# Two score pairs ahead of the last key tile's values, in front of six blocks of an attention and feed-forward kernel

## The chip, the cores and the metric

The kernel runs on one core of one Trainium2 chip. The metric is the device time of one execution in microseconds (us); less is better. Before the change the median of three runs is 1400.2 us (1399.88 to 1400.24).

## What is computed

Layer normalisation of x (2048 tokens, 512 features), softmax attention with 32 heads of 16 features on it, a gated feed-forward network of width 1792 on the same normalised x, and a gated sum. All data are 32-bit floats.

```python
def _A_ref(x, wqkv, wo):
    B, S, D = x.shape
    H = 32; Dh = D // H
    qkv = (lambda x, *d: x.transpose(*d))((x @ wqkv).reshape(B, S, 3, H, Dh), 2, 0, 3, 1, 4)
    q, k, v = qkv[0], qkv[1], qkv[2]
    scale = Dh ** -0.5
    scores = jnp.einsum("bhqd,bhkd->bhqk", q, k) * scale
    p = _softmax(scores, axis=-1)
    o = jnp.einsum("bhqk,bhkd->bhqd", p, v)
    return (lambda x, *d: x.transpose(*d))(o, 0, 2, 1, 3).reshape(B, S, D) @ wo

def _B_ref(x, w_gate, w_up, w_down):
    g = _silu(x @ w_gate)
    u = x @ w_up
    return (g * u) @ w_down

x = A_x
xn = _layernorm(x, axis=-1)
s = _A_ref(xn, A_wqkv, A_wo)
g = _silu(_B_ref(xn, B_w_gate, B_w_up, B_w_down))
return x + s * g
```

## The kernel before

**Stages.** A prologue normalises x and projects it to queries, keys and values. Then the attention runs for 32 units, each of one group of four heads and one block of 512 queries over 16 key tiles of 128 keys. A unit is cut into blocks of three to six key tiles, 101 blocks in all, counted here from 0. The feed-forward network, and after it most of the output projection, are cut into small portions that are laid between the attention's instructions. A short end finishes the last query block.

**One block** (`run`, from line 957 on) has two parts. In the first part, called the stage here, TensorE makes the block's scores and works off the block's share of feed-forward portions. In the second part, the values' stretch, it multiplies the probabilities with the values. The order is written out on the host: `events` gives each block a list of steps D, A, B and F at set places, `run` issues them in that order, and every engine then works through its own queue in order.

- **D** is a direct score pair (`scored`, lines 944 to 949): two matmuls, one on rows 0 to 63 of the array and one on rows 64 to 127, into the two halves of one of two score buffers (line 942), and an exponential on ScalarE from that buffer into a probability tile `pr` (line 948). Since there are two buffers, the third D has to wait for the exponential of the first, and so on. Each key tile has two pairs.
- **A and B** are the two halves of a copied score pair: one matmul into the spare bank `acc[1]` (also line 942, in the profile with the output `acc`), and a VectorE copy out of it into the probability tile (line 1001 for A, line 1007 for B). There is one spare bank, so each of these matmuls waits for the copy in front of it. The exponential of a copied pair comes at the end of the stage, from the probability tile (line 1015).
- **F** is one feed-forward pair (`fill(1)`): a matmul on each half of the array, into `bankx` and `banky` (`both`, line 188). A block gets 24 such pairs where the gate and up projections are at work and 21 (`3 * FG`) where the down projection is, until the feed-forward network is done at block 86 (`early` is 87); later blocks get 12 or 9.
- **Values** (`values`, line 405): for each key tile four matmuls, one per head, each with a stationary operand of 128 x 17 and an output at its own quarter of the partitions of `acc[0]`. The profile records each of them as two, so a key tile is x8 in its rows.

From block 87 on, `run` already uses another end: it issues the values of all key tiles but the last, then `begin` (the first two D of the next block), and then the values of the last key tile. The next block finds those two pairs in `begun` and leaves its first two D out of its list. In blocks 0 to 85 all values come first and the two D open the next block.

VectorE also has chores (splitting weights and hidden values into two parts, normalising finished units). `run` issues a chore after a step where its planned cost fits ahead of the next copy.

A block of six key tiles with 24 feed-forward pairs has 10 D and 2 copied pairs. One with 21 feed-forward pairs has 9 D and 3 copied pairs; its steps are D D F A F F F F D B F F D F F A F D F F F D B F F D F A F F D F F B D F. There are six such blocks: 7, 19, 40, 52, 73 and 85, each the second block of its unit. The block in front of each has five key tiles.

Of the kernel before, what the change touches and what calls it, by code (L numbers as in the profile page):

```python
# [33 lines left out]
FG = 7  # L34
# [18 lines left out]
def tile_block(ctx: ExitStack, tc: tile.TileContext, x, wqkv, wo, w_gate, w_up, w_down, out):  # L53
# [87 lines left out]
    def tidy(room=None):  # L141
        while chores and (room is None or chores[0][0] <= room):
            cost, work = chores.pop(0)
            work()
            if room is not None:
                room -= cost
# [19 lines left out]
    def catch_up():  # L166
        while after:
            after.pop(0)()
# [30 lines left out]
    def close():  # L199
        while closing:  # L200
            closing.pop(0)()
# [136 lines left out]
    def out_steps():  # L338
        if now == early:
            for c in range(DT - 1):  # L340
                load_out(0, c)
        if now == early + 1:
            for c in range(DT - 1):
                load_out(1, c)
            for t in range(NT):
                load_gates(t)
        if now == opened[units - 3] + 3:
            for c in range(DT - 1):
                load_out(2, c)
        if now == opened[units - 1] + 1:  # L350
            load_gate()

    def out_splits():
        for b, c in {early + 1: ((0, 0), (0, 1)), early + 2: ((0, 2),), early + 3: ((1, 0),), early + 4: ((1, 1),),
                     early + 6: ((1, 2),), early + 7: ((2, 0),), early + 8: ((2, 1),), early + 10: ((2, 2),)}.get(now, ()):
            split_out(b, c)
        if now - opened[units - 1] - 2 in range(EARLY):
            gate_rest(now - opened[units - 1] - 2)
# [42 lines left out]
    def values(u, kts, probs):  # L401
        for kt in kts:
            v = vst[(u // NB * NB + kt // CT) % RING]
            for h in range(4):
                mm(acc[0][h * 32:h * 32 + DH + 1], v[:, kt % CT, h * (DH + 1):(h + 1) * (DH + 1)],  # L405
                   probs[kt, h // 2][:, h % 2], start=kt == 0, stop=kt == KT - 1, skip_group_check=True)
# [59 lines left out]
    now = -1  # L466

    def fill(n):
        nonlocal given
        while n > 0 and queue:  # L470
            next(queue[0][0])
            queue[0][1] -= 1
            if not queue[0][1]:
                queue.pop(0)
            n -= 1
            given += 1

    sizes = []
# [4 lines left out]
    sizes = sizes[1:] + [3 * (DT - 1)] * EARLY + [3 * DT] * (NB * NT - NT)  # L483
    early = len(sizes) - EARLY - (NB * NT - NT)

    blocks, opened = [], []
# [19 lines left out]
    def events(n, f):  # L506
        length = 2 * n + f
        need = 2 * n - max(2, (10 * length + 46) // 40)
        fit = (10 * length + 55) // 112
        copied = max(0, min(need, fit)) if now else 0  # L510
        direct = 2 * n - copied
        gap = max(4, min(5, (length - 8) / max(1, direct - 2)))
        marks = [(0, "D"), (1, "D")] + [(7 + gap * i, "D") for i in range(direct - 2)]
        marks += [(2.2 + max(5.6, min(8, (length - 5) / (2 * copied))) * i, "AB"[i % 2]) for i in range(2 * copied)]
        marks.sort(key=lambda mark: mark[0] - 0.6 * (mark[1] == "D"))
        out = []
        at = left = 0
        for t, kind in marks:
            while left < f - (kind != "D") and at < t:
                out.append((at, "F"))  # L520
                left += 1
                at += 1
            out.append((at, kind))
            at += 1 if kind == "D" else 0.5
        return direct, out + [(at + i, "F") for i in range(f - left)]
# [409 lines left out]
    now = 0  # L935
# [3 lines left out]
    def scores(u, bank, kt, j, h):  # L939
        k, kc = kst[(u // NB * NB + kt // CT) % RING], kt % CT  # L940
        r = slice(h * HALF, h * HALF + NROW)
        mm(bank, k[r, j, kc * P:(kc + 1) * P], qst[u % 2][r, j], start=True, stop=True)  # L942

    def scored(u, slot, kt, j):
        for h in order():
            scores(u, score[slot][:, h], kt, j, h)
        pr = ppool.tile([P, 2, TB], F32, tag="pr", name="pr")
        act(pr, score[slot], AF.Exp, scale=0.25)  # L948
        return pr
# [3 lines left out]
    def begin(u, first, n):  # L953
        for j in range(2):
            begun[first, j] = scored(u, j, first, j)

    def run(u, first, n):
        nonlocal lower
        f = sizes.pop(0) if sizes else 0
        direct, todo = events(n, f)  # L960
        if now == 0:
            for _ in range(4):
                todo.insert(0, todo.pop(max(i for i, (_, e) in enumerate(todo) if e == "F")))
        pairs = [(kt, j) for kt in range(first, first + n) for j in range(2)]
        straight, copies = pairs[:direct], pairs[direct:]
        probs, waiting, turned_in = {}, [], []

        def unit_end():
            while ends:
                ends.pop(0)()  # L970
            out_steps()

        done = len(begun)
        if done:
            probs.update(begun)
            begun.clear()
            todo = [i for i in todo if i not in ((0, "D"), (1, "D"))]
            unit_end()
        copying = [t + 1.5 for t, e in todo if e in "AB"]
        final = max(at for at, (_, e) in enumerate(todo) if e == "F")  # L980
        free = 0
        for at, (t, e) in enumerate(todo):
            if at == final and not copying:
                tidy()
            if e == "F":
                fill(1)
            elif e == "D":
                probs[straight[done]] = scored(u, done % 2, *straight[done])
                done += 1
                if done == 2:  # L990
                    unit_end()
            elif e == "A":
                if now > early + 1 and not turned_in:
                    turned_in.append(now)
                    out_splits()
                kt, j = copies.pop(0)
                waiting.append((kt, j))
                scores(u, spare_bank, kt, j, 0)
                lower = True
                probs[kt, j] = ppool.tile([P, 2, TB], F32, tag="pr", name="pr")  # L1000
                dve.tensor_copy(probs[kt, j][:, 0], spare_bank)  # L1001
                free = copying.pop(0) + 3
            else:
                kt, j = waiting[-1]
                scores(u, spare_bank, kt, j, 1)
                lower = False
                dve.tensor_copy(probs[kt, j][:, 1], spare_bank)  # L1007
                free = copying.pop(0) + 3
            if not copying:
                close()  # L1010
            while chores and at < final and (not copying or max(free, t) + chores[0][0] <= copying[0] + 0.5):
                free = max(free, t) + chores[0][0]
                chores.pop(0)[1]()
        for kt, j in waiting:
            act(probs[kt, j], probs[kt, j], AF.Exp, scale=0.25)  # L1015
        tidy()
        if not turned_in:
            out_splits()
            tidy()
        catch_up()  # L1020
        kts = range(first, first + n)
        if early <= now + 1 < len(blocks):
            values(u, kts[:-1], probs)
            begin(*blocks[now + 1])
            values(u, kts[-1:], probs)
        else:
            values(u, kts, probs)

    for now, (u, first, n) in enumerate(blocks):
        g, b = divmod(u, NB)  # L1030
        if first == 0 and 0 < u < units - 1:
            load_q(u + 1)
            load_shift(u + 1)
        if now == 3 or first == 0 and 0 < g < NG - 1 and b == 0:
            load_k(g + 1, 0)
            load_v(g + 1, 0)
        run(u, first, n)
        if now == 0:
            load_k(0, NB - 1)
            load_v(0, NB - 1)  # L1040
        elif now == 1:
            load_q(1)
            load_shift(1)
        if b == NB - 1 and g + 1 < NG:
            for c in range(NB - 1):
                if first < (c + 1) * CT <= first + n:
                    load_k(g + 1, c + 1)
                    load_v(g + 1, c + 1)
        if first + n == KT and u + 1 < units:
            ends.append(partial(finish, u))  # L1050
# [81 lines left out]
```

## Time and profile before

| what | before |
|---|---|
| median of three runs | 1400.2 us (1399.88 to 1400.24) |
| the profiled execution's own time | 1399.78 us |
| its span (first to last recorded instruction) | 1398.0 us |
| granted TensorE clock, mean | 1.0 |
| TensorE matmul busy | 1391.3 us, 100% of the span |
| ScalarE busy | 1088.8 us, 78% |
| VectorE busy | 770.5 us, 55% |

In the rows, PE is TensorE's matmuls, PEld its weight loads, DVE is VectorE, ACT is ScalarE, POOL is GpSimd. L942 is line 942 of the kernel. A row of the timeline gives the start in us, the length in us, the engine, the line, the operation, output<-inputs with their shapes, and how many instructions were merged; in brackets stands how long the engine was idle before and who released it. TensorE's matmuls are pipelined and a new one starts before the last has ended, so a busy share of 100% does not say that nothing waits: one has to look at the distance from start to start.

### The profile page before, as it was taken

The page shows a single profiled execution, that of the slowest core. Times are in us where ns is not written, and L with a number is a line of the kernel's source. Part 1 is how long each engine was busy: PE and PEld are TensorE (multiplying, and loading weights), DVE is VectorE, ACT ScalarE, POOL GpSimd, SP SyncE. Part 2 cuts the span into 40 slices and gives each one's busy share as a digit, 9 for nine tenths or more (in the row PEclk, how much of TensorE's full clock was granted, in tenths as well). Part 3 has the DMA queues.
Part 4 walks back from the last instruction along what each step waited for, and adds up shares of the span by engine and source line. Part 5 has one row for each costly group of instructions (what it writes and reads, how often), then busy time and mean ns, then how long its engine had stood idle before and what let it go on. Part 6 is the DMA issues. An engine that isn't in the chain of part 4 may idle for free.

```text
span 1398.0 us, 27683 instructions
## 1 busy us (share of the span) xinstructions
PE 1391.3 (100%) x11193; PEld 842.4 (60%) x11193; DVE 770.5 (55%) x1301; ACT 1088.8 (78%) x1245; POOL 90.8 (6%) x104
## 2 busy tenths in 40 slices
PE   9999999999999999999999999999999999999998
PEld 7777755655665565566556556655565565565554
DVE  6674555455645653556446645554565446556555
ACT  6753678877888877787888778778877887788885
POOL 4200200000000000000000000000000000000333
PEclk9999999999999999999999999999999999999999
DMA  7768741043634511254514303356224123234433
GB/s 228 271 243 259 185 103 43 13 116 85 131 85 118 118 43 36 56 132 95 138 50 112 91 13 73 77 145 148 60 72 114 34 46 73 66 88 141 125 100 112
DMA packets 126954, 148.14 MB, mean 106 GB/s; under 512 B 12524, under 2 KB 79340, under 8 KB 126052
## 3 DMA queue, kind: packets, MB, share of 16 engines
q1 hardware_dynamic: 121620, 125.79, 35.1%
q0 software_dynamic: 4912, 20.12, 3.9%
q8 instruction: 89, 1.46, 0.4%
q14 instruction: 45, 0.37, 0.1%
q10 hardware_dynamic: 288, 0.39, 0.1%
HBM read 106.68 MB, written 39.58 MB: 105 GB/s over the span
## 4 chain that ended last, share of the span: by engine, by line
PE 88%; ACT 0%; DVE 0%; issue 0%; DVEq 0%
PE acc L405 32%; PE bankx L188 23%; PE score L942 17%; PE banky L188 12%; PE acc L942 3%; ACT pr L948 0%; PE acc L1069 0%; PE banky L1069 0%; PE score L1069 0%; DVE y L1076 0%; DVE y L1082 0%; DVEq L1128 0%
## 5 line engine op out<-in xcount | busy, mean ns | idle before, releaser
L948 ACT ACTIVATE pr<-score 128x1024 f32<-128x1024 f32 x856 | 810.4, 1031 | 228.5 <-PE score L942 226.3
L405 PE MATMUL acc<-pr,vst 128*17 128x512 f32 x4096 | 461.9, 593 | 0.0
L942 PE MATMUL score<-qst,kst 50*128 50x512 f32 x1712 | 391.0, 413 | 0.1
L188 PE MATMUL bankx<-fx,guh 64*128 64x512 f32 x896 | 333.5, 393 | 0.1
L188 PE MATMUL banky<-fx,guh 64*128 64x512 f32 x896 | 324.7, 393 | 0.0
L405 PEld LDWEIGHTS acc<-pr,vst 128*17 128x17 f32 x4096 | 108.7, 97 | 285.9 <-issue 262.2
L942 PEld LDWEIGHTS score<-qst,kst 50*128 50x128 f32 x1712 | 175.2, 184 | 148.1 <-issue 68.0
L1001 DVE COPY pr<-acc 128x512 f32<-128x512 f32 x168 | 116.3, 692 | 193.2 <-PE acc L942 191.4
L188 PE MATMUL bankx<-wd,hh 64*128 64x512 f32 x672 | 199.9, 392 | 0.0
L188 PE MATMUL banky<-wd,hh 64*128 64x512 f32 x672 | 197.4, 392 | 0.0
L188 PEld LDWEIGHTS bankx<-fx,guh 64*128 64x128 f32 x896 | 166.4, 186 | 18.7 <-issue 0.9
L188 PE MATMUL banky<-fx,gul 64*128 64x512 f32 x448 | 175.4, 391 | 0.0
L188 PE MATMUL bankx<-fx,gul 64*128 64x512 f32 x448 | 175.3, 391 | 0.0
L1015 ACT ACTIVATE pr<-pr 128x1024 f32<-128x1024 f32 x168 | 172.3, 1077 | 0.0
L188 PEld LDWEIGHTS banky<-fx,guh 64*128 64x128 f32 x896 | 166.4, 186 | 6.1
L1007 DVE COPY pr<-acc 128x512 f32<-128x512 f32 x168 | 116.2, 691 | 72.2 <-PE acc L942 61.3
L241 DVE SCALAR_TENSOR_TENSOR ga<-th,bankx 128x512 f32<-128x512 f32 x56 | 38.5, 688 | 178.4 <-ACT th L240 178.4
L942 PE MATMUL acc<-qst,kst 50*128 50x512 f32 x336 | 135.1, 402 | 0.0
L188 PEld LDWEIGHTS bankx<-wd,hh 64*128 64x128 f32 x672 | 125.0, 186 | 13.1
L188 PEld LDWEIGHTS banky<-wd,hh 64*128 64x128 f32 x672 | 124.4, 186 | 3.3
L188 PEld LDWEIGHTS bankx<-fx,gul 64*128 64x128 f32 x448 | 83.7, 187 | 10.3
L188 PEld LDWEIGHTS banky<-fx,gul 64*128 64x128 f32 x448 | 83.5, 186 | 3.7
(179 smaller groups left out, 1323.6 us busy)
## 6 DMA issues: line engine op xcount, KB each, us to landing
gur<-in_B_w_gate_dram SPq DMA_DIRECT2D x56, 256.0 KB
gur<-in_B_w_up_dram SPq DMA_DIRECT2D x56, 256.0 KB
wdr<-in_B_w_down_dram SPq DMA_DIRECT2D x56, 256.0 KB
kst<-k_d SPq DMA_DIRECT2D x192, 64.0 KB
qst<-q_d SPq DMA_DIRECT2D x192, 64.0 KB
fx<-xt_d SPq DMA_DIRECT2D x24, 512.0 KB
q_d<-parts SPq DMA_DIRECT2D x16, 512.0 KB
k_d<-parts SPq DMA_DIRECT2D x16, 512.0 KB
```

Source lines behind the costliest of these rows:

```text
L188: mm(banks[i], lhs[halves[i]], rhs[halves[i]], start=start, stop=stop)
L241: dve.scalar_tensor_tensor(ga, th, 1.0, bankx, op0=ALU.add, op1=ALU.mult)
L405: mm(acc[0][h * 32:h * 32 + DH + 1], v[:, kt % CT, h * (DH + 1):(h + 1) * (DH + 1)], probs[kt, h // 2][:, h % 2], start=kt == 0, stop=kt = ...
L942: mm(bank, k[r, j, kc * P:(kc + 1) * P], qst[u % 2][r, j], start=True, stop=True)
L948: act(pr, score[slot], AF.Exp, scale=0.25)
L1001: dve.tensor_copy(probs[kt, j][:, 0], spare_bank)
L1007: dve.tensor_copy(probs[kt, j][:, 1], spare_bank)
L1015: act(probs[kt, j], probs[kt, j], AF.Exp, scale=0.25)
```

## The change

The early start of the next block, used from block 87 on, is also used in front of every block of six key tiles whose share of the feed-forward work is 21 pairs.

```diff
         kts = range(first, first + n)
-        if early <= now + 1 < len(blocks):
+        if early <= now + 1 < len(blocks) or blocks[now + 1:] and blocks[now + 1][2] == 6 and sizes[0] == 3 * FG:
             values(u, kts[:-1], probs)
             begin(*blocks[now + 1])
             values(u, kts[-1:], probs)
         else:
             values(u, kts, probs)
```

It moves instructions at six places in TensorE's order, all of the same kind. The first of them, where block 6 ends and block 7 begins, stands in the following piece of the difference; `vst_549` and `vst_553` are values of key tiles 0 to 3 and of key tile 4, `score_8969` and `score_8970` are the two score buffers, and a row's x is the number of matmuls in the program.

```order
 L188 MATMUL banky<-wd,hh 128x512
 L405 MATMUL acc_80<-pr,vst_549 17x512 x16
-L405 MATMUL acc_80<-pr,vst_553 17x512 x4
 L942 MATMUL score_8969<-qst_556,kst_552 128x512 x2
 L942 MATMUL score_8970<-qst_556,kst_552 128x512 x2
+L405 MATMUL acc_80<-pr,vst_553 17x512 x4
 L188 MATMUL bankx<-wd,hh 128x512
 L188 MATMUL banky<-wd,hh 128x512
```

The four score matmuls of block 7's first two pairs now stand between the fourth and the fifth key tile's values instead of behind the fifth's.

On VectorE one place differs, in block 85. `fx<-wor` and `part<-pair` are chores, each a cast and a subtraction; `pr<-acc_81` are the copies of A (L1001) and B (L1007).

```order
 L193 SCALAR_TENSOR_TENSOR y<-th,y 128x512
 L1013 CAST fx<-wor 128x512
+L1001 COPY pr<-acc_81 128x512
 L1013 TENSOR_TENSOR fx<-wor,fx 128x512
-L1001 COPY pr<-acc_81 128x512
+L1007 COPY pr<-acc_81 128x512
 L1013 CAST part<-pair 128x512
-L1007 COPY pr<-acc_81 128x512
+L1001 COPY pr<-acc_81 128x512
 L1013 TENSOR_TENSOR part<-pair,part 128x512
-L1001 COPY pr<-acc_81 128x512
 L1007 COPY pr<-acc_81 128x512
```

The three chores behind the first cast each move back by one copy. The order of the instructions on ScalarE, GpSimd and SyncE, and so of all their DMAs, is the same as before.

## Prediction

> **What bounds the kernel now.** I begin with the page's first and fourth part, the busy times and the chain that ended last.
>
> ```profile
> PE 1391.3 (100%) x11193; PEld 842.4 (60%) x11193; DVE 770.5 (55%) x1301; ACT 1088.8 (78%) x1245; POOL 90.8 (6%) x104
> PE 88%; ACT 0%; DVE 0%; issue 0%; DVEq 0%
> ```
>
> TensorE carries 88% of the chain and no other engine 1%. So what counts is how TensorE's starts follow each other around the six places, and whether ScalarE, at 78%, holds it up there.
>
> Second view: the busy times in stretches, one for each stage, from the end of one values' stretch to the start of the next as the timeline gives them. The first six are the stages of blocks 7, 19, 40, 52, 73 and 85, which the change prepares earlier. Then come block 8 (five key tiles, 21 pairs), block 10 (six, 24 pairs) and block 11 (five, 24 pairs). The first number behind the colon pair is the length.
>
> ```profile
> 245.92:254.23 8.31, 8.31 (x67) 6.83 (x67) 3.83 (x6) 7.61 (x9) 0.00 (x0) 1.00 0.00 0
> 399.64:407.78 8.14, 8.14 (x67) 6.77 (x66) 3.81 (x6) 7.54 (x8) 0.26 (x1) 1.00 0.09 34
> 669.64:677.76 8.12, 8.12 (x67) 6.76 (x66) 3.81 (x6) 7.51 (x8) 0.13 (x1) 1.00 0.91 234
> 823.47:831.76 8.29, 8.29 (x67) 6.82 (x66) 3.81 (x6) 7.60 (x9) 0.00 (x0) 1.00 0.00 0
> 1093.42:1101.70 8.28, 8.28 (x66) 6.79 (x66) 3.81 (x6) 7.61 (x9) 0.00 (x0) 1.00 0.01 2
> 1247.21:1255.38 8.17, 8.17 (x67) 6.81 (x67) 5.10 (x9) 7.54 (x8) 0.13 (x1) 1.00 0.20 64
> 259.57:267.02 7.45, 7.45 (x63) 5.82 (x62) 2.77 (x4) 6.91 (x8) 0.00 (x0) 1.00 0.00 0
> 283.45:292.08 8.63, 8.63 (x73) 6.67 (x73) 3.97 (x6) 8.10 (x9) 0.00 (x0) 1.00 0.60 148
> 297.43:305.56 8.13, 8.13 (x69) 6.39 (x69) 3.61 (x6) 7.60 (x9) 0.00 (x0) 1.00 0.48 109
> ```
>
> Three feed-forward pairs cost 8.13 - 7.45 = 0.68 us, 0.23 each. A stage of six key tiles with 21 pairs should then last 8.63 - 0.68 = 7.95 us. The six last 0.36, 0.19, 0.17, 0.34, 0.33 and 0.22 us longer, 1.61 us together. That is all that an earlier start can win in these stages.
>
> Which engine causes it? Third view: who waited for whom within the stage of block 7, the three rows of the answer in which TensorE waits.
>
> ```profile
> PEld score L942 <- issue: 0.8, 1, 0.8
> PEld acc L405 <- issue: 0.4, 1, 0.4
> PEld acc L942 <- DVE pr L1007: 0.3, 1, 0.3
> ```
>
> The one wait on another engine is a spare-bank score on VectorE's copy. No score waits for an exponential. Short waits may be missing here, so I test it with a twin: block 94 opens with the same twenty steps (D D F A F F F F D B F F D F F A F D F F) and already has its two first pairs ahead of the last values. Fourth view, the timelines of block 7 and of block 94, TensorE's score and spare-bank rows with the ScalarE and VectorE rows that matter:
>
> ```profile
> 246.45 6.66 ACT L948 ACTIVATE pr<-score 128x1024 f32<-128x1024 f32 x7 [2.48 <-PE score L942]
> 253.28 1.94 ACT L948 ACTIVATE pr<-score 128x1024 f32<-128x1024 f32 x2 [0.17 <-PE score L942]
> 247.16 0.69 DVE L1001 COPY pr<-acc 128x512 f32<-128x512 f32 x1 [4.14 <-PE acc L942]
> 247.57 0.47 PE L942 MATMUL score<-qst,kst 50*128 50x512 f32 x1
> ...
> 247.90 0.49 PE L942 MATMUL acc<-qst,kst 50*128 50x512 f32 x1
> ...
> 248.51 0.59 PE L942 MATMUL score<-qst,kst 50*128 50x512 f32 x2
> ...
> 249.24 0.43 PE L942 MATMUL acc<-qst,kst 50*128 50x512 f32 x1
> ...
> 249.63 0.52 PE L942 MATMUL score<-qst,kst 50*128 50x512 f32 x2
> ```
>
> ```profile
> 1331.54 2.96 ACT L948 ACTIVATE pr<-score 128x1024 f32<-128x1024 f32 x3 [1.11 <-PE score L942]
> 1330.38 0.69 DVE L1001 COPY pr<-acc 128x512 f32<-128x512 f32 x1 [3.06 <-PE acc L942]
> 1329.88 0.39 PE L942 MATMUL acc<-qst,kst 50*128 50x512 f32 x1
> ...
> 1330.82 0.40 PE L942 MATMUL score<-qst,kst 50*128 50x512 f32 x1
> ...
> 1331.12 0.50 PE L942 MATMUL acc<-qst,kst 50*128 50x512 f32 x1
> ...
> 1331.75 0.57 PE L942 MATMUL score<-qst,kst 50*128 50x512 f32 x2
> ...
> 1332.45 0.45 PE L942 MATMUL acc<-qst,kst 50*128 50x512 f32 x1
> ...
> 1332.85 0.53 PE L942 MATMUL score<-qst,kst 50*128 50x512 f32 x2
> ```
>
> In block 94 ScalarE has a head start and runs dry for 1.11 us; in block 7 it works through seven exponentials without a pause. If ScalarE held block 7 up, block 94 would get ahead. Counted from the first A (246.66, row below, and 1329.88), the rows come in block 7 after 0.91, 1.24, 1.85, 2.58 and 2.97 us and in block 94 after 0.94, 1.24, 1.87, 2.57 and 2.97 us. That is the same pace within 0.03 us. What both share is the spare bank: the B at +1.24 starts just as the copy of A ends (247.16 + 0.69 = 247.85 before the start at 247.90; 1330.38 + 0.69 = 1331.07 before 1331.12). I take the chain of spare bank and VectorE copies as the cause of the 1.61 us. The change leaves its place behind the first F as it is.
>
> **The switch between values and scores.** Per place nothing is added or removed; four score matmuls move ahead of one key tile's values. Before, TensorE goes values, scores, feed-forward; afterwards values, scores, values, feed-forward. The price is in the trace, since block 86 ends in the new form and block 6 in the old, both with five key tiles. Fifth view, TensorE's timeline around both:
>
> ```profile
> 241.43 4.49 PE L405 MATMUL acc<-pr,vst 128*17 128x512 f32 x40
> 245.85 0.74 PE L942 MATMUL score<-qst,kst 50*128 50x512 f32 x4
> ...
> 246.66 0.39 PE L942 MATMUL acc<-qst,kst 50*128 50x512 f32 x1
> ```
>
> ```profile
> 1268.16 3.63 PE L405 MATMUL acc<-pr,vst 128*17 128x512 f32 x32
> 1271.72 0.72 PE L942 MATMUL score<-qst,kst 50*128 50x512 f32 x4
> 1272.38 1.05 PE L405 MATMUL acc<-pr,vst 128*17 128x512 f32 x8
> ...
> 1273.69 0.40 PE L942 MATMUL acc<-qst,kst 50*128 50x512 f32 x1
> ```
>
> From the first values to the first A, the same work lies in between: 40 values, two pairs, one F. It takes 246.66 - 241.43 = 5.23 us in the old form and 1273.69 - 1268.16 = 5.53 us in the new. The new form costs **0.30 us**, six times **1.80 us**.
>
> Two pages of the Trainium skill speak to this and disagree. "TensorE: Matmul & The Clock Gate", Part 2, step 5 (NX overlap), says that one matmul's drain is hidden under the next one's fill; by it the order would cost nothing, and the six places would add 0. "TensorEngine Tiling (Array Packing)", section Key Properties, says that changing the tiling mode drains the engine; values use quarters of the columns and scores halves of the rows, so two more changes a place would cost something. The 0.30 us go with the second.
>
> **What the earlier start wins.** The scores come 1.97 us ahead of the first A (1271.72 to 1273.69) instead of 0.81 us (245.85 to 246.66), so ScalarE gets 1.16 us more. By the twin this is worth 0 us, by the other end 1.61 us. I take 0, to which the twin's rows are nearest.
>
> **The rest.** The chores of block 85: a subtraction now stands between the copies of A and of B. Block 87 has this order already:
>
> ```profile
> 1274.13 0.69 DVE L1001 COPY pr<-acc 128x512 f32<-128x512 f32 x1 [1.87 <-PE acc L942]
> 1274.73 0.68 DVE L1013 TENSOR_TENSOR fx<-wor,fx 128x512 fp32r<-128x512 f32 x1
> 1275.40 0.69 DVE L1007 COPY pr<-acc 128x512 f32<-128x512 f32 x1
> ```
>
> The copies start 1.27 us apart there, and A and B 1.24 us apart in block 7, so the subtraction fits under the wait for B: 0 us. If it did not, VectorE's later copies would be late by at most the subtraction's 0.68 us. VectorE's first copy after a pause differs between the six stages: three of them lose about 0.34 us and three about 0.19. If the shift moved one group to the other, that would be 3 x 0.15 = 0.45 us either way. I take 0. Exponentials of the copied pairs, loads and stores keep their order, and ScalarE only gets earlier: 0 us.
>
> **Sum.** 6 x 0.30 - 0 + 0 = +1.8 us on the profiled execution's 1399.78 us, 1401.6 us. The median of the runs shown is 0.4 us above that execution, so I predict a median of **1402.0 us**, +0.13%. About 0.2% (2.8 us) is what a measurement of this kernel can tell from no change, so this is within it. With the terms at 0 open by 0.45 us either way, the forecast's own range is 1401.5 to 1402.5.
>
> **Rivals.**
> - *The excess is ScalarE's.* Then the 1.61 us go and the switches stay: 1.80 - 1.61 = +0.2 us, 1400.4. For it: ScalarE is busy 7.61 of 8.31 us in block 7's stage and without a pause for seven exponentials. Against: the twin's pace. 14%.
> - *The spare-bank chain tightens; slower.* B starts 0.05 us behind the end of A's copy in block 7 and in block 94 alike, so there is no slack. If the copies start 0.15 us later behind the cut values' stretch (the difference between the two groups of stages), B waits that much longer, and so do two later ones. Three such waits in six stages are 18 x 0.15 = 2.7 us, with the switches 4.5 us: 1404.7. It decides once the distance from A to B passes 1.3 us. Against: block 94 keeps 1.24. 8%.
> - *The switches cost nothing here and the excess goes*: -1.6 us, 1398.6. This is what the first of the two pages would allow. Against: block 86's 5.53 us. 4%.
> - The change not doing what it says is ruled out by the order of the instructions: six places, nothing else on TensorE.
>
> **How the numbers follow.** The forecast has 71%, the rivals 14, 8 and 4%, and 3% remain for what I do not see. The range takes in the forecast and the first rival, 1400.4 at the low end, and at the high end half a microsecond beyond the forecast's own, for a subtraction that is not hidden: 1403.0. It leaves out the second and third rival. Within 0.2% (1397.4 to 1403.0) lie forecast, first and third rival, and half of the rest: 0.88. Slower by more is the second rival with some of the rest: 0.10. Faster by more needs 2.8 us where at most 1.61 us are to be had: 0.02.
>
> **What would show it.** In the profile of the changed kernel the values in front of the six blocks stand as x32, scores x4, values x8, and from the first values to the first A are 5.53 us, not 5.23. ScalarE shows a pause of about a microsecond behind its first two exponentials there. The six stretches from the first A to the next values keep their length within 0.1 us. If these get shorter by 0.2 to 0.4 us each, ScalarE was the cause after all; if the A to B distance goes beyond 1.3 us, the second rival holds.

## The result and the profile after

| what | before | after |
|---|---|---|
| median | 1400.24 us (22 runs, 1399.64 to 1401.42) | 1402.07 us (22 runs, 1401.58 to 1403.75) |
| the profiled execution's own time | 1399.78 us | 1402.24 us |
| its span | 1398.0 us | 1400.2 us |

The ratio is 1.0014 with a 95% interval of 1.0008 to 1.002: the change costs 1.8 us, 0.13%. That is less than the 0.2% named ahead, but with 22 runs each it is a small loss, not nothing.

The page of the changed kernel looks like that of before: TensorE, ScalarE and VectorE have the same work, and TensorE carries the chain.

```profile
PE 1393.8 (100%) x11193; PEld 841.7 (60%) x11193; DVE 770.5 (55%) x1301; ACT 1089.1 (78%) x1245; POOL 91.0 (6%) x104
PE 88%; ACT 0%; DVE 0%; issue 0%; DVEq 0%
```

TensorE's timeline of the changed kernel around the end of block 6, beside the rows of before in the prediction:

```profile
241.70 3.63 PE L405 MATMUL acc<-pr,vst 128*17 128x512 f32 x32
245.26 0.73 PE L942 MATMUL score<-qst,kst 50*128 50x512 f32 x4
245.92 1.05 PE L405 MATMUL acc<-pr,vst 128*17 128x512 f32 x8
...
247.25 0.39 PE L942 MATMUL acc<-qst,kst 50*128 50x512 f32 x1
...
248.49 0.50 PE L942 MATMUL acc<-qst,kst 50*128 50x512 f32 x1
```

The values are cut into x32 and x8 with the scores between them. From the first values to the first A now lie 247.25 - 241.70 = 5.55 us instead of 5.23: 0.32 us more for the same instructions.

The weight loads around this place in the changed kernel show something that the prediction did not look at:

```profile
245.26 0.30 PEld L942 LDWEIGHTS score<-qst,kst 50*128 50x128 f32 x4 [0.85 <-issue]
245.92 0.13 PEld L405 LDWEIGHTS acc<-pr,vst 128*17 128x17 f32 x8 [0.36 <-issue]
246.91 0.18 PEld L188 LDWEIGHTS bankx<-wd,hh 64*128 64x128 f32 x1 [0.85 <-issue]
...
247.01 0.19 PEld L942 LDWEIGHTS acc<-qst,kst 50*128 50x128 f32 x1
```

At each change of kind (245.26, 245.92, 246.91) the first weight load starts together with its matmul. Where the kind stays the same it starts ahead: the load of the A at 247.01, for its matmul at 247.25.

The head start has come, too. ScalarE's timeline in the changed kernel, block 7:

```profile
245.87 1.94 ACT L948 ACTIVATE pr<-score 128x1024 f32<-128x1024 f32 x2 [1.62 <-PE score L942]
248.89 6.92 ACT L948 ACTIVATE pr<-score 128x1024 f32<-128x1024 f32 x7 [1.09 <-PE score L942]
```

ScalarE does the first two exponentials early and then stands idle for 1.09 us, since the third score pair comes no sooner than before: 0.94 us behind the first A here, 0.91 in the kernel before. Whether TensorE gained anything behind the first A is read from the busy times in stretches from the first A to the next values, in the six stages. First the kernel before, then the changed kernel (the number behind the stretch is its length, ACT the fourth busy time):

```profile
246.66:254.23 7.57, 7.57 (x63) 6.22 (x59) 3.83 (x6) 7.40 (x9) 0.00 (x0) 1.00 0.00 0
400.37:407.78 7.41, 7.41 (x62) 6.17 (x58) 3.81 (x6) 7.28 (x8) 0.00 (x0) 1.00 0.10 38
670.37:677.76 7.39, 7.39 (x62) 6.16 (x58) 3.81 (x6) 7.25 (x8) 0.00 (x0) 1.00 0.89 231
824.20:831.76 7.56, 7.56 (x62) 6.22 (x58) 3.81 (x6) 7.40 (x9) 0.00 (x0) 1.00 0.00 0
1094.15:1101.70 7.55, 7.55 (x62) 6.18 (x58) 3.81 (x6) 7.40 (x9) 0.00 (x0) 1.00 0.01 2
1247.95:1255.38 7.43, 7.43 (x62) 6.20 (x59) 4.74 (x8) 7.27 (x8) 0.00 (x0) 1.00 0.22 67
```

```profile
247.25:254.80 7.55, 7.55 (x62) 6.22 (x58) 3.81 (x6) 6.31 (x8) 0.00 (x0) 1.00 0.00 0
401.24:408.65 7.41, 7.41 (x63) 6.12 (x59) 3.83 (x6) 6.13 (x7) 0.00 (x0) 1.00 0.07 24
671.48:678.88 7.40, 7.40 (x63) 6.17 (x59) 3.81 (x6) 6.10 (x7) 0.00 (x0) 1.00 0.86 223
825.63:833.22 7.59, 7.59 (x63) 6.10 (x59) 3.83 (x6) 6.35 (x8) 0.00 (x0) 1.00 0.00 0
1095.98:1103.55 7.57, 7.57 (x62) 6.14 (x58) 3.82 (x6) 6.32 (x8) 0.00 (x0) 1.00 0.01 2
1250.09:1257.53 7.44, 7.44 (x62) 6.19 (x58) 5.34 (x9) 6.12 (x7) 0.00 (x0) 1.00 0.17 50
```

ScalarE has 1.1 us less to do in each stretch, and the lengths are the same within 0.03 us. One row of the waits in block 7's stage of the changed kernel names what is still waited for, the same as before:

```profile
PEld acc L942 <- DVE pr L1007: 0.3, 1, 0.3
```

### The profile page after: what moved, and what is told of

Read it like the earlier page. It is cut to its first block, busy times and chain, and to the rows that moved or that the text cites. A ratio compares the mean times of both kernels' runs of the same rounds, so it can differ in the third digit from the quotient of the medians.

```text
span 1400.2 us, 27683 instructions
## 1 busy us (share of the span) xinstructions
PE 1393.8 (100%) x11193; PEld 841.7 (60%) x11193; DVE 770.5 (55%) x1301; ACT 1089.1 (78%) x1245; POOL 91.0 (6%) x104
## 4 chain that ended last, share of the span: by engine, by line
PE 88%; ACT 0%; DVE 0%; issue 0%; DVEq 0%
PE acc L405 32%; PE bankx L188 25%; PE score L942 17%; PE banky L188 11%; PE acc L942 3%; ACT pr L948 0%; PE acc L1069 0%; PE banky L1069 0%; PE score L1069 0%; DVE y L1076 0%; DVE y L1082 0%; DVEq L1128 0%
## 5 line engine op out<-in xcount | busy, mean ns | idle before, releaser
L1001 DVE COPY pr<-acc 128x512 f32<-128x512 f32 x168 | 116.2, 692 | 195.6 <-PE acc L942 191.9
L1007 DVE COPY pr<-acc 128x512 f32<-128x512 f32 x168 | 116.2, 691 | 71.4 <-PE acc L942 61.0
```

## The experiments

Theory: each place costs the change from values to scores and back, 0.3 us, and the six stages lose their time to the chain of spare bank and VectorE copies. Rival: they lose it to ScalarE. In the diffs `...` stands for lines left out. The kernel before had medians of 1400.2 to 1400.29 us beside these runs.

**The early start everywhere.** The switch price, 83 times more.

```diff
-        if early <= now + 1 < len(blocks):
+        if 3 <= now and now + 1 < len(blocks):
```

> The kernel before, with the early start in front of every block from block 4 on: 83 places more than before (97 instead of 14). Switch theory (each place costs 0.30 us of TensorE time, and ScalarE holds no stage up): +25 us, 1425 us, and each of the 83 places shows the same 0.3 us. ScalarE theory (the early start pays where ScalarE is nearly full, and the stages with 24 pairs have ten exponentials in 8.6 us): the stages get shorter by some tenths each, so clearly less than +25 us, at 0.2 us each +8 us or less.

Measured: 1426.3 us, ratio 1.0185 (1.017 to 1.0201). Against 1400.26 us that is 26.0 us for 83 places, 0.31 us each. In the trace, block by block from one values' stretch to the next, 82 of the 83 blocks from 4 to 86 are 0.27 to 0.36 us longer than before (one 0.22), whether they have 24 or 21 feed-forward pairs, and the others differ by at most 0.03. So the price holds at every one of these places, and at none of them is ScalarE's head start worth anything that shows.

**Half of each copy.** In the six blocks VectorE's copies are cut to half their columns.

```diff
...
+        w = TB // 2 if six else TB
...
-                dve.tensor_copy(probs[kt, j][:, 0], spare_bank)
+                dve.tensor_copy(probs[kt, j][:, 0, :w], spare_bank[:, :w])
```

> The kernel before, but in the six blocks VectorE copies only the left half of the columns of each spare-bank score (256 of 512); the exponentials of the copied pairs take that half, and the values read it twice, so half of these probabilities are left out. Spare-bank theory: a copy takes about 0.35 instead of 0.69 us, no spare-bank score waits any more, the six stages fall from 8.31, 8.14, 8.12, 8.29, 8.28, 8.17 to about 7.95 us each, -1.6 us in all (1398.6). ScalarE theory: the stages stay as they are, 0 us (1400.2).

Measured: 1398.15 us, ratio 0.9986 (0.9977 to 0.9995), 2.1 us faster. The six stages in this kernel, from the end of one values' stretch to the start of the next:

```profile
246.32:254.24 7.92, 7.92 (x68) 6.40 (x67) 2.49 (x6) 7.38 (x8) 0.00 (x0) 1.00 0.00 0
399.59:407.47 7.88, 7.88 (x67) 6.25 (x67) 2.46 (x6) 7.41 (x8) 0.24 (x1) 1.00 0.09 35
669.33:677.19 7.86, 7.86 (x67) 6.31 (x67) 2.47 (x6) 7.38 (x8) 0.10 (x1) 1.00 0.92 237
822.90:830.79 7.89, 7.89 (x68) 6.54 (x67) 2.46 (x6) 7.35 (x8) 0.00 (x0) 1.00 0.00 0
1092.52:1100.42 7.90, 7.90 (x66) 6.34 (x66) 2.45 (x6) 7.37 (x8) 0.00 (x0) 1.00 0.01 2
1245.97:1253.87 7.90, 7.90 (x67) 6.36 (x67) 3.74 (x9) 7.42 (x8) 0.11 (x1) 1.00 0.19 66
```

In five of the six stages VectorE is busy for 2.5 instead of 3.8 us (in block 85, with its chores, 3.7 instead of 5.1), ScalarE for 7.4 instead of 7.5 to 7.6, and the difference between the two groups of stages (8.3 and 8.15 before) is all but gone. A half copy takes 0.42 us, not the 0.35 expected. The shorter exponentials of the copied pairs do not count here: they start behind the first values (255.11 against 254.23 in block 7 before). The copies are the cause.

**Half of each exponential.** The same cut on ScalarE instead.

```diff
...
+        w = TB // 2 if now in six else TB
...
-        act(pr, score[slot], AF.Exp, scale=0.25)
+        act(pr[:, :, :w], score[slot][:, :, :w], AF.Exp, scale=0.25)
```

> The kernel before, but in the six blocks the exponential of each direct pair takes only the left half of the columns (256 of 512 of each score), and the values read it twice, so half of these probabilities are left out. ScalarE is then busy for well under half of the stage. Spare-bank theory: the six stages stay within 0.1 us of 8.31, 8.14, 8.12, 8.29, 8.28, 8.17, 0 us in all (1400.2). ScalarE theory: they fall to about 7.95 us each, -1.6 us in all (1398.6).

Measured: 1400.36 us, ratio 1.0002 (0.9993 to 1.0011). The stages in this kernel:

```profile
245.93:254.24 8.31, 8.31 (x66) 6.88 (x66) 3.82 (x6) 4.75 (x9) 0.00 (x0) 1.00 0.00 0
399.69:407.86 8.17, 8.17 (x68) 6.90 (x67) 3.82 (x6) 4.74 (x9) 0.25 (x1) 1.00 0.09 34
669.84:677.98 8.14, 8.14 (x66) 6.91 (x67) 3.81 (x6) 4.74 (x9) 0.12 (x1) 1.00 0.85 219
823.65:831.94 8.29, 8.29 (x67) 6.78 (x67) 3.81 (x6) 4.74 (x9) 0.00 (x0) 1.00 0.00 0
1093.63:1101.93 8.30, 8.30 (x67) 6.86 (x66) 3.82 (x6) 4.75 (x9) 0.00 (x0) 1.00 0.01 2
1247.49:1255.66 8.17, 8.17 (x67) 6.88 (x67) 5.10 (x9) 4.75 (x9) 0.12 (x1) 1.00 0.19 64
```

ScalarE's busy time falls from 7.6 to 4.75 us of the stage, and no stage gets shorter. This pair of runs settles the rival: a busy share of over 90% in a stage was not what held it.

**One B moved.** `events` gets the same steps, but the second B stands ahead of its D (the numbers are the places of A and B among the D and F behind the two first D; the second B had 17).

```diff
-        return direct, out + [(at + i, "F") for i in range(f - left)]
+        out += [(at + i, "F") for i in range(f - left)]
+        if now > 0 and n == 6 and f == 3 * FG:
+            kinds, put, at, seen = [e for _, e in out if e not in "AB"], [], 0, 0
+            for i, e in enumerate(kinds[2:] + [""]):
+                if i in (1, 6, 11, 16, 21, 26):
+                    put.append((at + 2, "AB"[seen % 2]))
+                    seen, at = seen + 1, at + 0.5
...
+            out = out[:2] + put
+        return direct, out
```

> The kernel before, with one step moved in the six blocks: the second B (the fourth spare-bank score) comes ahead of the D in front of it instead of behind, so that all five distances between spare-bank scores are 5.5 steps instead of 5.5, 5.5, 6.5, 4.5, 5.5. Spare-bank theory: the wait at the fifth spare-bank score goes, about 0.2 us in each stage, -1.2 us in all (1399.0); at least half of that. ScalarE theory: 0 us (1400.2), or a little slower, since nothing is changed for the exponentials.

Measured: 1399.01 us, ratio 0.9991 (0.9982 to 1.0), 1.25 us lower, with no change just inside the interval. Three of its six stages, blocks 7, 19 and 40:

```profile
246.02:254.16 8.14, 8.14 (x68) 6.90 (x67) 3.81 (x6) 7.52 (x8) 0.00 (x0) 1.00 0.00 0
399.56:407.56 8.00, 8.00 (x68) 6.87 (x67) 3.82 (x6) 7.50 (x8) 0.25 (x1) 1.00 0.09 35
669.47:677.46 7.99, 7.99 (x67) 6.90 (x67) 3.83 (x6) 7.51 (x8) 0.12 (x1) 1.00 0.90 233
```

Each of the six is 0.13 to 0.17 us shorter than in the kernel before, so the trace shows about 0.9 us; the rest of the 1.25 is not seen in it. The reason is in the five turns of the spare bank. In block 7 before, the fifth score follows the end of the copy in front of it by 0.05 us and the fourth by 0.34 us; with the moved B these distances are 0.14 and 0.10 us.

**The moved B in the changed kernel.**

> The changed kernel with the same moved B as in e4_even. If switch price and spare-bank chain are two separate terms: 1402.1 - 1.25 = 1400.8 us, that is e4_even plus 1.8 us. ScalarE theory in its last form (the early start pays once the spare bank no longer masks it): the stages fall further than in e4_even, to 7.5 us, and the time comes to e4_even's 1399.0 us or below.

Measured: 1401.19 us, ratio 1.0005 (0.9996 to 1.0014). That is 2.2 us above the moved B alone, where 1.8 was expected, on another chip. In block 7 values and stage together last 12.96 us in this profile and 12.63 in that of the moved B alone, 0.33 more, and over the six places it is 1.85 us. From the first A to the next values block 7 takes 7.42 us here and 7.40 without the early start, so the head start gains nothing. The switch price is paid in full also where the spare bank waits less.

**The two pairs apart.** Another two changes at each of the six places.

```diff
-            values(u, kts[:-1], probs)
-            begin(*blocks[now + 1])
+            ...
+                values(u, kts[:-2], probs)
+                begun[first1, 0] = scored(u1, 0, first1, 0)
+                values(u, kts[-2:-1], probs)
+                begun[first1, 1] = scored(u1, 1, first1, 1)
             values(u, kts[-1:], probs)
```

> The changed kernel, but at its six places the two score pairs stand apart: values of all key tiles but two, first pair, values of the last but one, second pair, values of the last. Twice as many changes between values and scores. If each change has a fixed price (0.30 us for two of them): +1.8 us on the changed kernel, 1403.9. If the price is made of single distances (values to score 0.52 instead of 0.41 us, score to score behind it 0.33 instead of 0.23, score to values 0.32): the second of these falls away when a pair stands alone, and a pair alone costs 0.21 us, two of them 0.42 instead of 0.31: +0.7 us, 1402.7.

Measured: 1404.15 us, ratio 1.0026 (1.0016 to 1.0037): 2.1 us above the changed kernel. The fixed price is right; my piecewise account fell. TensorE's timeline at the end of block 6 in this kernel shows why:

```profile
241.81 2.77 PE L405 MATMUL acc<-pr,vst 128*17 128x512 f32 x24
244.51 0.50 PE L942 MATMUL score<-qst,kst 50*128 50x512 f32 x2
244.94 1.05 PE L405 MATMUL acc<-pr,vst 128*17 128x512 f32 x8
245.93 0.50 PE L942 MATMUL score<-qst,kst 50*128 50x512 f32 x2
246.36 1.05 PE L405 MATMUL acc<-pr,vst 128*17 128x512 f32 x8
...
247.68 0.39 PE L942 MATMUL acc<-qst,kst 50*128 50x512 f32 x1
```

From a lone pair to the values behind it are 244.94 - 244.51 = 0.43 us, not 0.32 as I had assumed, and from two pairs in the changed kernel 245.92 - 245.26 = 0.66 us. The second pair adds one distance of 0.23 us, the rest is paid once for each visit. From the first values to the first A are 247.68 - 241.81 = 5.87 us, another 0.32; counted by whole blocks, the six places are 0.31 to 0.36 us longer than in the changed kernel.

**No early start at all.** Is it worth its price in the late blocks, where it was from the start?

```diff
-        if early <= now + 1 < len(blocks):
+        if False:
```

> The kernel before without any early start: the 14 places from the end of block 86 on are undone as well. If the early start only costs its switches there too: -14 x 0.31 = -4.3 us, 1395.9. If the short stages of blocks 87 to 100 (12 or 9 feed-forward pairs, five or six exponentials) wait for ScalarE without it, that is given back: 1400 us or more, and the values of the last key tiles, or the scores, wait for exponentials in the profile.

Measured: 1400.77 us, ratio 1.0003 (0.9994 to 1.0012). The saved switches are given back. Block by block, six of the 14 places save 0.16 to 0.36 us (behind 86, 89, 91 and 97 to 99) and eight lose 0.04 to 0.29 us (behind 87, 88, 90 and 92 to 96), 0.5 us lost in all. Two values' stretches of this kernel show why: that of block 93 with four key tiles, here with ScalarE's row beside it, and that of block 97 with three.

```profile
1326.21 4.19 PE L405 MATMUL acc<-pr,vst 128*17 128x512 f32 x32
1327.31 2.00 ACT L1015 ACTIVATE pr<-pr 128x1024 f32<-128x1024 f32 x2
```

```profile
1369.81 2.90 PE L405 MATMUL acc<-pr,vst 128*17 128x512 f32 x24
```

x32 takes 3.63 us where nothing waits (block 86 before), so the first waits for 0.56 us; x24 takes 2.77 us (block 93 before), so the second waits for 0.13. The last key tile's probabilities come late there: in block 93 the last exponential ends at 1327.31 + 2.00 = 1329.31, and the values that need it start at 1329.36. The early start fills this wait with the next block's scores: it pays where the wait is longer than 0.31 us, and costs where it is shorter.

**The six spare-bank scores placed anew.** Same code as the moved B, with the places 0, 5, 11, 16, 22, 27.

> The kernel before with all six spare-bank scores of the six blocks placed anew: the first A straight behind the two first D, and distances of 5.5, 6.5, 5.5, 6.5, 5.5 steps. Spare-bank theory: against e4_even the wait at the third and at the fifth goes too, the stages of blocks 7, 52 and 73 come down to those of 19, 40 and 85: up to 0.4 us less than e4_even, 1398.6 to 1399.0. If the last B, which now stands one step later, delays the values or their exponentials, it is slower than e4_even.

Measured: 1400.16 us, ratio 0.9997 (0.9988 to 1.0006): no better than before, and 1.15 us behind the moved B. ScalarE's timeline of block 7 in this kernel:

```profile
246.69 8.65 ACT L959 ACTIVATE pr<-score 128x1024 f32<-128x1024 f32 x9 [2.50 <-PE score L953]
```

All nine exponentials now stand in one row, where block 7 of the kernel before had a pause behind the seventh. From the third spare-bank score on, each has 0.16 us or more behind the end of the copy in front of it. But the fourth to the ninth D start 0.05 to 0.24 us behind the end of the exponential that frees their buffer (0.11 to 0.38 before). The first B, now ahead of the third D, holds that D up (248.02 us, 1.93 behind the first D, against 1.72 before), and ScalarE has no time left to make it good. I read from this that ScalarE is the next limit in these stages, close behind the spare bank; no run tests it by itself.

**The late places chosen.** The early start stays where the last values wait.

```diff
-        if early <= now + 1 < len(blocks):
+        if early <= now < len(blocks) - 1 and (n == 4 or f == 9):
```

> The kernel before, with the early start kept only behind those late blocks whose values wait for exponentials without it: 8 of the 14 places (behind blocks 87, 88, 90, 92 to 96; four key tiles, or 9 feed-forward pairs), and undone behind 86, 89, 91 and 97 to 99. Cover theory (the scores are worth their switches only where they fill a wait of the last values): the place behind block 86 gives back 0.31 us and the other five 0.18 us each (stage and values 7.29 us in the run without any early start, 7.47 in the kernel before), -1.2 us, 1399.1. Head-start theory (what counts is ScalarE's earlier begin of the next stage): undoing places costs time, 1400.3 us or more.

Measured: 1398.63 us, ratio 0.9989 (0.998 to 0.9998), 1.6 us faster. In the trace the six undone places give 1.2 us, as expected; another 0.24 us is gone from the stage of block 88, in front of which the early start was kept, and why is open. Undoing places saves time; the head-start theory is out here as well.

**Both.** The chosen late places with the moved B.

> The same choice of late places together with the moved B of e4_even in the six blocks. If both terms add: -1.25 - 1.2 us, 1397.8 us, faster than the kernel before and the changed kernel.

Measured: 1397.43 us, ratio 0.9981 (0.9972 to 0.999), 2.8 us faster than the kernel before and 4.6 us faster than the changed kernel. The two terms add: 1.25 and 1.6.

## Why the prediction was right, point by point

- **What holds the six stages.** The spare-bank chain, as the twin block had shown: half copies give 2.1 us, half exponentials 0. The size was low. I put the loss at 1.61 us from feed-forward pairs at 0.23 us; without the copies' wait the stages last 7.86 to 7.92 us, not 7.95, so it is 1.96 us in the stages.
- **The switch.** 0.30 us a place was read from block 86; measured 0.30 to 0.34 at the six places, 0.31 over 83 places, and about as much again when it is paid twice. Two pages of the Trainium skill were weighed. "TensorEngine Tiling (Array Packing)", Key Properties (a change of mode drains the engine), agrees with the runs in that changes cost time: with 12 changes 1.8 us, with 24 changes 3.9 us more than before. The overlap of the Trainium skill's "TensorE: Matmul & The Clock Gate", Part 2, step 5, agrees with the trace within one kind of matmul (two feed-forward pairs start 0.23 us apart at 0.39 us each) and not at these changes (from values to a score 0.52 us, from values to values 0.41). No run tells a drain from the weight loads that begin only with their matmul at each change.
- **The head start.** Predicted 0 us with a pause of about a microsecond on ScalarE; measured 0.03 us at most and 1.09 us.
- **The chores of block 85.** Predicted 0 us; the stretch behind block 85's first A is 7.44 us against 7.43.
- **The open term.** The two groups of stages stayed as they were. Why three of them lose 0.15 us more than the others was not tested by itself; since half copies all but remove the difference, it lies in the spare-bank chain. The trace says where: in blocks 7, 52 and 73 the copy of the first A starts 0.50 us behind the start of its matmul, in the other three 0.43 or 0.44 us, so the first turn lasts 1.24 to 1.25 against 1.17 to 1.18 us; the last turn differs by as much. What makes VectorE start later there is open.
- **The rivals.** ScalarE as the cause fell with the half exponentials. A tighter spare-bank chain would have shown the first A to B beyond 1.3 us. In block 7 of the changed kernel it is 248.49 - 247.25 = 1.24 us as before (last two rows of the first timeline above), and in the six stages 1.17 to 1.24 us. Free switches fell with the same timeline.
- **The sum.** 1402.0 us predicted, 1402.07 measured. That is closer than the runs can bear out, since the interval of the ratio spans 1.1 to 2.8 us; the terms of the sum, seen place by place, carry the account. The six places give 6 x 0.32 = 1.9 us of the 2.2 us between the two profiled spans.

## What to carry to other kernels

An engine that is busy for over 90% of a stage need not hold it up: look for a twin stage in the same trace in which that engine has a head start, and compare the pace. Interleaving two kinds of matmul has a price per visit, readable from the trace, so a visit must fill a wait that is longer than the price; here it did so behind some late blocks and nowhere else. Where one buffer goes round between two engines, spacing its uses evenly in the order can be worth more than starting anything earlier.

## What the runs showed of the hardware

- A visit of TensorE to another kind of matmul between the values (128x17 operands at the four quarters of the output's partitions, against 64-row halves) costs 0.31 us on the average of 83 places, whether it makes one score pair or two: in front of block 7 a visit with both pairs costs 0.32 us, and two visits with one pair each cost another 0.32. The first weight load behind each change starts together with its matmul, where otherwise it starts ahead (246.91 and 247.01 in the changed kernel).
- One turn of the spare bank, score matmul 0.39 us and copy of 128x512 0.69 us, with the hand-overs between them, takes 1.17 to 1.35 us from start to start where the next score follows the end of the copy by 0.05 us (246.66 to 247.90, 1.24 us, in block 7 before). Before the change this was so in the first, the fourth and the fifth of a stage's five turns; the second and third had 0.12 us or more to spare. Moving a single B by one place was worth 0.13 to 0.17 us in each stage.
